# A linear attention and its feed-forward layers on one core: where the activation's last step writes, whose banks y and the state updates use, and a new order of the work

## The chip, the cores and the metric

The kernel runs on one core of a Trainium2 chip. The metric is the device time of one execution in microseconds (us), as a median of several runs; lower is better. A core has five engines, each with its own queue of instructions that it works off in order: PE (matrix products, with weight loads as PEld), DVE and POOL (elementwise), ACT (functions and copies) and SP (here it issues all transfers). They wait for one another by semaphores. Data lies in SBUF; PE writes its sums to PSUM, which has eight banks of 128 rows x 512 floats.

## What is computed

Attention with a decaying state per head, then a feed-forward pair of layers with an activation of its own:

```python
batch, n_heads, seq, head_dim = (4, 8, 768, 48)
...
for t in range(S):
    kt, vt, rt = (k[:, :, t], v[:, :, t], r[:, :, t])
    cur = np.einsum('bhd,bhe->bhde', u[None] * kt, vt)
    y[:, :, t] = np.einsum('bhd,bhde->bhe', rt, state + cur)
    state = w[None, :, :, None] * state + np.einsum('bhd,bhe->bhde', kt, vt)
...
h = x @ w_in                      # x [3072, 384], w_in [384, 2048]
sp = np.maximum(h, 0.0) + np.log1p(np.exp(-np.abs(h)))
g = h * erf(sp)
return (g @ w_out).astype(np.float32)      # w_out [2048, 384]
```

x is y with the heads side by side. The weights come as 64-bit floats (the kernel sees them as int64).

## The kernel before

**Chunks and blocks.** The attention runs over 24 chunks of 128 tokens; chunk g belongs to batch g % 4, and chunks 4b to 4b+3 make up block b, 512 tokens (`TB`), of the six blocks of the layers. For a chunk, PE multiplies r and k, which were scaled by powers of w (`prep_r` L222, `prep_k` L218), to A in two banks (`a_step`, PE at L301); DVE copies the masked A into `am` (L309, for chunks 0 and 1 L314) over a diagonal that comes from r, u and k (`diag_a` L263, `diag_b` L266, `diag_c` L270, `diag_m`); PE makes y from `am`, v and the state `sbd` (`y_product`, PE at L330) and the state's update ds from k and v (`ds_product`, PE at L353; k is scaled for it by `prep_n`, L226); DVE adds ds into the state (`s_add` L366, L368) and `s_mul` (L372) multiplies the state by the decay. `x_hi` (ACT, L375) and `x_lo` (DVE, L378; for some chunks ACT, L392) copy y as a high and a low part into x. Chunks 0 and 1 are "direct": they load less (below), POOL or DVE makes their product r*k (`prep_g`, L231), PE turns k (`turn_k`), and DVE makes the diagonal from that (`diag_v`, L253).

**Layers.** 96 layer steps n, each 128 hidden units (f) of one block: units 0 to 7 for blocks 0 and 1, then 8 to 15 for these, then 16 for each of blocks 2 to 5. Of each step, f1 is nine matmuls into a bank h of pool `ps3` (`f1`, PE at L411: high x high, high x low, low x high, three times); then a (ACT, tanh, L418), b (ACT, tanh, L422), z (DVE, L427), c, d, e (ACT, L431, L435, L439), g (DVE, L443), h (ACT, the high part `gh`, L449), l (DVE, the low part `gl`, L454), and f2, called p in the order, nine matmuls into the three sums `acc` (PE at L471).

**Weights.** Each of the two matrices comes in eight pieces of 768 columns (`WG`; 768 KB each). A piece takes six steps, `load_w` a to f: a on ACT (L123, from the raw words into the one buffer `wt`), b, c, d on DVE (L125, L127, L130, bits into `wt`), e on ACT (L133, the high part), f on DVE or POOL (L135, the low part). There is one buffer `wt` (`WTB`), so a piece's a waits for the f of the piece before it; there are two buffers for the raw words.

**PSUM.** `ps1` holds the three sums, `psa` two banks (tag "A"), `ps3` three (tag "h"). For chunks 0 to 3, y lies in a bank of `ps1` and ds in one of `ps3`; from chunk 4 on both lie in `psa`, where A lies too (but for chunks 0 and 2, whose A is in `ps3`). Banks of a pool are given out in turn, so a new tile waits for the last use of the tile that had its bank.

**What sets the order.** A string `ORDER` of tokens, one for each step: within the scheduler's manual mode each engine works its instructions off in the order of the tokens. L is the load of a chunk (a: r and k, 512 KB; b: the rest, 608 KB, of the direct chunks 224 KB), U that of u (192 KB), F the fetch and C the steps of a weight piece (C13d: `w_out`, piece 3, step d), R, K, N, G, Q and M the preparations of a chunk, V turn_k, A, P (masked copies), Y, D (ds), X and S as above; f, a, b, z, c, d, e, g, h, l, p with the number of the layer step; O the copy and store of sums, W dummy matmuls that keep PE busy, Z the count below, T, t, B and H the tables of powers of w. A "+" behind a token puts it on POOL, a "*" on ACT. SP issues the loads in the same order, all in one queue.

**The count.** `count_bad` compares w with its range (DVE), sums the differing entries with a tiny matmul (PE) and reduces that (DVE); the count decides, behind everything, whether a general version of the kernel runs after (it doesn't with these inputs).

The activation's last step before:

```python
def act_g(n):
    h = ff[n]["h"]
    nc.vector.scalar_tensor_tensor(out=h, in0=ff[n]["s"], scalar=FC, in1=h, ...)
```

## Time and profile before

| | us |
|---|---|
| three runs | 513.9, 515.3, 515.69 |
| median | 515.3 |
| profiled execution, its own time | 513.87 |
| span in that profile | 511.8 |
| granted TensorE clock in it | 0.997 of full |

Busy in the profiled execution:

| engine | busy us | share | instructions |
|---|---|---|---|
| PE | 496.6 | 97% | 4476 |
| PEld | 391.8 | 77% | 4476 |
| DVE | 357.4 | 70% | 642 |
| ACT | 390.4 | 76% | 712 |
| POOL | 135.7 | 27% | 135 |

The span is from the first to the last recorded instruction; some 2 us of the execution lie around it. A row of a time line gives the start, how long the instruction took (or a run of like ones, "x24"), the engine, the line of the kernel, the operation and its tiles as out<-in, and in brackets how long the engine idled before it and what it waited for. A busy PE is not the same as PE at its peak, since matmuls overlap: their modelled ends reach into the next one's start.

### The profile page before, as it was taken

How to read it: one execution, taken by the hardware profiler on the slowest of the kernel's cores; microseconds unless marked ns; L12 is line 12 of the kernel's file. 1: busy time of each engine (PE TensorE's matmuls, PEld its weight loads, DVE VectorE, ACT ScalarE, POOL GpSimd, SP SyncE). 2: the span in 40 equal slices, each digit the busy share in tenths (PEclk: the TensorE clock that was granted, in tenths of full speed). 3: DMA queues.
4: the chain of work that ended last, by engine and by line, in shares of the span. 5: the costliest groups of instructions: out<-in, count | busy, mean ns of one | idle time of the engine just before them, and what ended most of it. 6: DMA issues, size and time to landing. Idle time of an engine off the chain costs nothing.

```text
span 511.8 us, 11055 instructions
## 1 busy us (share of the span) xinstructions
PE 496.6 (97%) x4476; PEld 391.8 (77%) x4476; DVE 357.4 (70%) x642; ACT 390.4 (76%) x712; POOL 135.7 (27%) x135
## 2 busy tenths in 40 slices
...
GB/s 276 363 195 119 249 125 62 243 176 153 224 12 42 2 260 96 131 20 73 2 1 215 49 1 86 97 36 167 22 131 1 1 2 3 41 22 0 0 1 67
DMA packets 13993, 48.16 MB, mean 94 GB/s; under 512 B 1776, under 2 KB 2160, under 8 KB 13936
## 3 DMA queue, kind: packets, MB, share of 16 engines
...
q14 instruction: 20, 0.16, 0.1%
...
## 4 chain that ended last, share of the span: by engine, by line
PE 85%; DVE 5%; DMA 4%; ACT 3%; SPq 1%; issue 1%; ACTq 0%
PE acc L471 38%; PE h L411 37%; PE y L330 6%; PE A L301 3%; DMA out_dram<-o 2%; DMA raw<-in_win_dram 1%; PE ds L353 1%; DMA att<-in_att_dram 1%; DVE wt L130 1%; DVE wt L127 1%; DVE am L309 1%; DVE gl L454 1%; ACT s L435 0%; SPq L72 0%; ACT s L422 0%
## 5 line engine op out<-in xcount | busy, mean ns | idle before, releaser
L411 PE MATMUL h<-x,wih 128*128 128x512 f32 x576 | 184.8, 402 | 1.0 <-DVE gl L454 0.9
L411 PEld LDWEIGHTS h<-x,wih 128*128 128x128 f32 x576 | 106.4, 188 | 29.3 <-DVE gl L454 3.2
L471 PE MATMUL acc<-gh,woh 128*128 128x512 f32 x288 | 116.0, 403 | 0.0
L411 PE MATMUL h<-x,wil 128*128 128x512 f32 x288 | 114.3, 397 | 0.0
L471 PE MATMUL acc<-gh,wol 128*128 128x512 f32 x288 | 114.2, 397 | 0.0
L471 PE MATMUL acc<-gl,woh 128*128 128x512 f32 x288 | 114.1, 396 | 0.0
L427 DVE SCALAR_TENSOR_TENSOR s<-s,h 128x512 f32<-128x512 f32 x96 | 65.2, 683 | 46.8 <-ACT s L422 46.2
L454 DVE TENSOR_TENSOR gl<-h,gh 128x512 fp32r<-128x512 f32 x96 | 66.0, 689 | 39.8 <-ACT gh L449 38.3
L443 DVE SCALAR_TENSOR_TENSOR h<-s,h 128x512 f32<-128x512 f32 x96 | 66.0, 691 | 37.9 <-ACT s L439 37.3
L449 ACT CAST gh<-h 128x512 fp32r<-128x512 f32 x96 | 55.8, 582 | 36.1 <-DVE h L443 20.6
L418 ACT ACTIVATE s<-h 128x512 f32<-128x512 f32 x96 | 56.9, 593 | 27.5 <-PE h L411 27.1
L431 ACT ACTIVATE s<-s 128x512 f32<-128x512 f32 x96 | 60.0, 627 | 22.7 <-DVE s L427 22.4
L471 PEld LDWEIGHTS acc<-gh,woh 128*128 128x128 f32 x288 | 54.2, 188 | 14.2 <-issue 0.8
L411 PEld LDWEIGHTS h<-x,wil 128*128 128x128 f32 x288 | 54.3, 188 | 13.3 <-DVE wil L135 0.3
L471 PEld LDWEIGHTS acc<-gh,wol 128*128 128x128 f32 x288 | 54.3, 188 | 13.1
L471 PEld LDWEIGHTS acc<-gl,woh 128*128 128x128 f32 x288 | 54.3, 189 | 12.5
L422 ACT ACTIVATE s<-s 128x512 f32<-128x512 f32 x96 | 60.4, 630 | 1.7
L435 ACT ACTIVATE s<-s 128x512 f32<-128x512 f32 x96 | 60.4, 630 | 1.7
L439 ACT ACTIVATE s<-s 128x512 f32<-128x512 f32 x96 | 60.1, 629 | 1.7
L283 POOL TENSOR_TENSOR am<-idents,q 128x512 f32<-128x512 f32 x25 | 28.5, 1150 | 76.6 <-PE y L330 65.5
L309 DVE COPY_PREDICATED am<-mask,A 64x128 f32<-64x128 uint32 (+2 forms) x108 | 38.3, 389 | 3.0 <-PE A L301 1.9
L222 POOL TENSOR_TENSOR att<-att,wr 112x512 f32<-112x512 f32 x16 | 21.8, 1363 | 42.8 <-DMA att<-in_att_dram 42.8
...
## 6 DMA issues: line engine op xcount, KB each, us to landing
...
```

The source lines that it names most:

```text
L309: nc.vector.copy_predicated(out=o, data=ap[rows, n, :, i], mask=mask[rows, n, None, i].to_broadcast(list(o.shape)).bitcast(U32))
L411: nc.tensor.matmul(out=h, lhsT=w[:, f, q, :], rhs=x[:, xi, q, :], start=k == 0, stop=k == 8)
L418: nc.scalar.activation(out=s1, in_=e["h"], func=AF.Tanh, bias=FB0, scale=FA0)
L422: nc.scalar.activation(out=s1, in_=s1, func=AF.Tanh, bias=FB1, scale=FA1)
L427: nc.vector.scalar_tensor_tensor(out=e["s"], in0=e["s1"], scalar=FG, in1=e["h"], op0=ALU.mult, op1=ALU.add)
L431: nc.scalar.activation(out=s, in_=s, func=AF.Tanh, bias=FB2, scale=FA2)
L435: nc.scalar.activation(out=s, in_=s, func=AF.Square, bias=FB3, scale=FA3)
L439: nc.scalar.activation(out=s, in_=s, func=AF.Square, bias=FB4, scale=FA4)
L443: nc.vector.scalar_tensor_tensor(out=h, in0=ff[n]["s"], scalar=FC, in1=h, op0=ALU.subtract, op1=ALU.mult, reverse0=True)
L449: nc.scalar.copy(out=e["gh"], in_=e["h"])
L454: eng.tensor_tensor(out=e["gl"], in0=e["h"], in1=e["gh"].bitcast(F32), op=ALU.subtract)
L471: nc.tensor.matmul(out=acc[e], lhsT=w[:, f, es], rhs=g, start=first and i == 0, stop=last and i == 2)
```

## The change

Five things change. Step g writes its result over `s` in SBUF, in place of its bank h; steps h and l read it there. y of chunk 4 and later, and ds of all chunks, lie in `ps3` beside the layers' h, in place of `psa`. The first piece of `w_in` is fetched and split in two halves of 384 columns (tokens F00 and F08, C00 and C08), in the same raw and `wt` buffers. The count is split in three tokens (Z0a, Z0b, Z0c). And `ORDER` is another string: it has the same steps, but their sequence differs nearly everywhere, and several of a chunk's preparations, several weight steps f and some masks change between DVE, POOL and ACT. The diff, cut:

```diff
+    halves = {int(x[1]) for x in ORDER.split() if x[0] == "F" and x[2] == "8"}
+
+    def columns(which, g):
+        if which in halves and g in (0, 8):
+            return 0, slice(0, WG // 2) if g == 0 else slice(WG // 2, WG)
+        return g, slice(g * WG, (g + 1) * WG)
 
     def fetch_w(which, g):
-        raws[which, g] = raw = stage.tile([P, WG], I64, tag="raw", name=f"raw{which}{g}")
-        nc.sync.dma_start(out=raw, in_=(wout if which else win)[:, g * WG:(g + 1) * WG])
+        n, s = columns(which, g)
+        if n == g:
+            raws[which, n] = stage.tile([P, WG], I64, tag="raw", name=f"raw{which}{n}")
+        nc.sync.dma_start(out=raws[which, n][:, s.start - n * WG:s.stop - n * WG],
+                          in_=(wout if which else win)[:, s])
 
     bits = {}
 
     def load_w(part, eng, which, g):
-        words = raws[which, g].bitcast(I32).rearrange("p (n two) -> p n two", two=2)
+        n, s = columns(which, g)
+        own = slice(s.start - n * WG, s.stop - n * WG)
+        words = raws[which, n][:, own].bitcast(I32).rearrange("p (n two) -> p n two", two=2)
         wl, wh = words[:, :, 0], words[:, :, 1]
-        if part == "a":
-            bits[which, g] = stage.tile([P, WG], I32, tag="wt", name=f"wt{which}{g}", bufs=WTB)
-        t = bits[which, g]
+        if part == "a" and n == g:
+            bits[which, n] = stage.tile([P, WG], I32, tag="wt", name=f"wt{which}{n}", bufs=WTB)
+        t = bits[which, n][:, own]
...
         s["y"] = y_product(chunks[g], [s["am", 0], s["am", 1]], g % 4, g < 4, f"y{g}", g in direct,
-                           (ps1, f"acc{g % 2}") if g < 4 else (psa, "A"))
+                           (ps1, f"acc{g % 2}") if g < 4 else (ps3, "h"))
...
-    def ds_product(t, first, name):
-        ds = (ps3 if first else psa).tile([PR, NPAIR, D], F32, tag="h" if first else "A", name=name)
+    def ds_product(t, home, name):
+        ds = home[0].tile([PR, NPAIR, D], F32, tag=home[1], name=name)
...
     def act_g(n):
-        h = ff[n]["h"]
-        nc.vector.scalar_tensor_tensor(out=h, in0=ff[n]["s"], scalar=FC, in1=h, op0=ALU.subtract, op1=ALU.mult,
+        s = ff[n]["s"]
+        nc.vector.scalar_tensor_tensor(out=s, in0=s, scalar=FC, in1=ff[n]["h"], op0=ALU.subtract, op1=ALU.mult,
                                        reverse0=True)
 
     def act_h(n):
         e = ff[n]
         e["gh"] = fp.tile([P, TB], F32R, tag="gh", name=f"gh_{n}")
-        nc.scalar.copy(out=e["gh"], in_=e["h"])
+        nc.scalar.copy(out=e["gh"], in_=e["s"])
 
     def act_l(n, eng):
         e = ff[n]
         e["gl"] = fp.tile([P, TB], F32R, tag="gl", name=f"gl_{n}")
-        eng.tensor_tensor(out=e["gl"], in0=e["h"], in1=e["gh"].bitcast(F32), op=ALU.subtract)
+        eng.tensor_tensor(out=e["gl"], in0=e["s"], in1=e["gh"].bitcast(F32), op=ALU.subtract)
...
+    def count_bad(part):
+        if part == "a":
+            bad_["in"] = bad = const.tile([PR, NPAIR], F32, name="bad")
+            nc.vector.tensor_tensor(out=bad, in0=wp[:, 0, 0], in1=wc, op=ALU.not_equal)
+        elif part == "b":
+            bad_["out"] = cnt = psa.tile([1, NPAIR], F32, tag="A", name="cnt")
+            nc.tensor.matmul(out=cnt, lhsT=wr[:, 0, 0:1], rhs=bad_["in"], start=True, stop=True)
+        else:
+            nc.vector.tensor_reduce(out=fi, in_=bad_["out"], axis=AX.X, op=ALU.max)
...
-            st_.setdefault(num, {})["ds"] = ds_product(chunks[num], num < 4, f"ds{num}")
+            st_.setdefault(num, {})["ds"] = ds_product(chunks[num], (ps3, "h"), f"ds{num}")
...
-P101 g26 M111+ f28 a28 p24y p24z b28 z28 h26 l26 z27 c27 d27 p25 A11 f29 e27 a29 P110 P111 Y11 D11 g27 h27 l27 c28 d28
...
+p26 f29 a29 M110+ N11+ M111+ g28 Y10 D10 A11 h28 b29 h27 L12a L12b O232c S10a S10b l27 z29 f30 X10a c29 a30 b30 d29
```

Three places of the sequence follow; numbers behind a tile's name tell tiles of one name apart, except that `wt03` is piece 3 of `w_in`, `wt12` piece 2 of `w_out`, and so on, `h0`, `s1_0`, `s2_0`, `gh_0`, `gl_0` belong to layer step 0, and `att4`, `am4`, `A4` to chunk 4.

DVE at the first piece of `w_in`, before (chunks 0 to 3 around it):

```order
L314 TENSOR_TENSOR am0_0_217<-A0_0_191,mask_99 128x512
L314 TENSOR_TENSOR am0_1_219<-A0_1_192,mask_99 128x512
L127 SCALAR_TENSOR_TENSOR wt00_186<-raw00_172,wt00_186 128x768
L253 TENSOR_TENSOR att0_167<-att0_167,kt0_202 128x4x48 x2
L130 SCALAR_TENSOR_TENSOR wt00_186<-raw00_172,wt00_186 128x768
L253 TENSOR_TENSOR att1_170<-att1_170,kt1_237 128x4x48 x2
L314 TENSOR_TENSOR am1_0_249<-A1_0_224,mask_99 128x512
```

and after:

```order
L137 SCALAR_TENSOR_TENSOR wt00_185<-raw00_176,wt00_185 128x384
L273 TENSOR_TENSOR att2_172<-att2_172,ub_90 128x384
L140 SCALAR_TENSOR_TENSOR wt00_185<-raw00_176,wt00_185 128x384
L145 TENSOR_TENSOR wil_95<-wt00_185,wih_94 128x384
L263 TENSOR_TENSOR att1_169<-att1_169,kt1_232 128x4x48 x2
L376 TENSOR_TENSOR sbd_147<-ds0_277,wp_114 48x4x48 x2
L324 TENSOR_TENSOR am1_0_330<-A1_0_298,mask_99 128x512
L324 TENSOR_TENSOR am1_1_332<-A1_1_299,mask_99 128x512
L135 TENSOR_SCALAR wt00_185<-wt00_185 128x384
```

Before, one b, c, d of 768 columns stand there, and the piece's f comes later, with ten rows between its d and it; now steps b, c, d of the first half (384 columns) stand there, its f (L145) is the next instruction after its d (L140), and the second half's b comes after two masked copies of chunk 1.

DVE around the first g and l of the layers, before:

```order
L226 TENSOR_TENSOR att4_406<-att4_406,wkn_146 128x384
L309 COPY_PREDICATED am4_0_543<-mask_99,A4_0_580 128x512
L309 COPY_PREDICATED am4_1_545<-mask_99,A4_1_581 128x512
L443 SCALAR_TENSOR_TENSOR h0_570<-s2_0_621,h0_570 128x512
L427 SCALAR_TENSOR_TENSOR s2_1_671<-s1_1_666,h1_598 128x512
L427 SCALAR_TENSOR_TENSOR s2_2_676<-s1_2_673,h2_625 128x512
L454 TENSOR_TENSOR gl_0_680<-h0_570,gh_0_678 128x512
L309 COPY_PREDICATED am5_0_608<-mask_99,A5_0_641 128x512
```

and after:

```order
L276 TENSOR_TENSOR att6_541<-att6_541 128x384
L453 SCALAR_TENSOR_TENSOR s2_0_625<-s2_0_625,h0_580 128x512
L437 SCALAR_TENSOR_TENSOR s2_1_671<-s1_1_666,h1_610 128x512
L135 TENSOR_SCALAR wt01_674<-wt01_674 128x768
L137 SCALAR_TENSOR_TENSOR wt01_674<-raw01_544,wt01_674 128x768
L140 SCALAR_TENSOR_TENSOR wt01_674<-raw01_544,wt01_674 128x768
L464 TENSOR_TENSOR gl_0_685<-s2_0_625,gh_0_680 128x512
L232 TENSOR_TENSOR att6_541<-att6_541,wr_115 112x512
```

The g of step 0 (L443, now L453) wrote `h0` and now writes `s2_0`; its l (L454, now L464) reads `h0` and `gh_0` before, `s2_0` and `gh_0` after. Before, the z of steps 1 and 2 stand between them; now one z and three steps of weight piece 1.

ACT from the instruction behind the high part of piece 2 of `w_out` (the twelfth piece; L133, `woh`) to the first step of piece 3 (the thirteenth; L123), before:

```order
L418 ACTIVATE s1_7_1070<-h7_1059 128x512
L422 ACTIVATE s1_7_1070<-s1_7_1070 128x512
L431 ACTIVATE s2_6_1053<-s2_6_1053 128x512
L449 CAST gh_5_1116<-h5_951 128x512
L435 ACTIVATE s2_6_1053<-s2_6_1053 128x512
L439 ACTIVATE s2_6_1053<-s2_6_1053 128x512
L375 CAST x1_755<-y7_1081 128x3x128
L431 ACTIVATE s2_7_1114<-s2_7_1114 128x512
L435 ACTIVATE s2_7_1114<-s2_7_1114 128x512
L439 ACTIVATE s2_7_1114<-s2_7_1114 128x512
L449 CAST gh_6_1165<-h6_1024 128x512
L123 ACTIVATE wt13_1169<-raw13_1047 128x768
```

and after, from that high part (L143) on:

```order
L143 CAST woh_96<-wt12_1111 128x768
L441 ACTIVATE s2_6_1136<-s2_6_1136 128x512
L428 ACTIVATE s1_7_1152<-h7_1101 128x512
L432 ACTIVATE s1_7_1152<-s1_7_1152 128x512
L445 ACTIVATE s2_6_1136<-s2_6_1136 128x512
L428 ACTIVATE s1_8_1158<-h8_1141 128x512
L449 ACTIVATE s2_6_1136<-s2_6_1136 128x512
L133 ACTIVATE wt13_1161<-raw13_1127 128x768
```

Before, eleven instructions stand between the two; now six do: the steps of layer step 6 (c, d, e), of 7 (a, b) and the a of step 8.

## Rows read from the trace of the kernel before

**Rows 1.** The page's busy time of each engine, and traffic in its 40 slices.

```profile
PE 496.6 (97%) x4476; PEld 391.8 (77%) x4476; DVE 357.4 (70%) x642; ACT 390.4 (76%) x712; POOL 135.7 (27%) x135
...
GB/s 276 363 195 119 249 125 62 243 176 153 224 12 42 2 260 96 131 20 73 2 1 215 49 1 86 97 36 167 22 131 1 1 2 3 41 22 0 0 1 67
```

**Rows 2.** Stretches: us, busy time (count) of PE, PEld, DVE, ACT, POOL, PE clock, DMA.

```profile
30.00:60.00 30.00, 26.05 (x395) 19.25 (x396) 28.94 (x48) 25.12 (x48) 16.34 (x12) 1.00 0.54 192
60.00:85.00 25.00, 25.00 (x183) 19.78 (x183) 21.54 (x31) 21.38 (x37) 15.11 (x13) 1.00 0.37 128
...
110.00:500.00 390.00, 389.80 (x3213) 310.85 (x3212) 255.96 (x460) 302.20 (x544) 84.06 (x83) 1.00 0.18 63
```

**Rows 3.** Time line of PE: start, us, line, operation, [idle before <-releaser].

```profile
52.71 0.73 PE L411 MATMUL h<-x,wih 128*128 128x512 f32 x2 [0.79 <-DVE gl L454]
...
56.42 0.86 PE L330 MATMUL y<-att,sbd 112*32 112x128 f32 x24 [0.86 <-DVE am L309]
...
58.09 0.50 PE L471 MATMUL acc<-gh,woh 128*128 128x512 f32 x1
...
66.20 0.40 PE L411 MATMUL h<-x,wil 128*128 128x512 f32 x1
...
84.45 0.39 PE L471 MATMUL acc<-gh,woh 128*128 128x512 f32 x1
...
88.76 0.90 PE L301 MATMUL A<-att 48*64 48x128 f32 x32
```

**Rows 4.** Time line of DVE and of POOL: the weights' last steps.

```profile
64.83 1.08 DVE L135 TENSOR_TENSOR wil<-wt,wih 128x768 fp32r<-128x768 f32 x1
...
82.57 1.84 POOL L135 TENSOR_TENSOR wol<-wt,woh 128x768 fp32r<-128x768 f32 x1 [3.50 <-ACT woh L133]
```

**Rows 5.** Time line of ACT and of DVE: where the weights' steps waited.

```profile
10.35 0.90 ACT L123 ACTIVATE wt<-raw 128x768 f32<-128x768 f32 x1 [3.85 <-DMA raw<-in_win_dram]
...
11.28 0.56 DVE L125 TENSOR_SCALAR wt<-wt 128x768 int32<-128x768 int32 x1 [0.93 <-ACT wt L123]
...
60.23 0.69 DVE L125 TENSOR_SCALAR wt<-wt 128x768 int32<-128x768 int32 x1 [0.75 <-ACT wt L123]
...
75.06 0.55 DVE L270 TENSOR_REDUCE q<-att 128x8 f32<-128x384 f32 x1 [0.44 <-POOL att L266]
```

**Rows 6.** Time line of POOL and DVE: instructions that overlap, and two that don't.

```profile
17.37 1.59 POOL L218 TENSOR_TENSOR att<-att,wk 112x512 f32<-112x512 f32 x1
...
17.75 1.63 DVE L266 TENSOR_TENSOR att<-att 128x384 f32<-128x384 f32 x1
...
21.00 0.55 DVE L266 TENSOR_TENSOR att<-att 128x384 f32<-128x384 f32 x1
21.46 0.95 DVE L135 TENSOR_TENSOR wil<-wt,wih 128x768 fp32r<-128x768 f32 x1
...
57.41 1.84 POOL L135 TENSOR_TENSOR wol<-wt,woh 128x768 fp32r<-128x768 f32 x1
...
57.47 0.69 DVE L454 TENSOR_TENSOR gl<-h,gh 128x512 fp32r<-128x512 f32 x1
...
67.02 1.21 DVE L125 TENSOR_SCALAR wt<-wt 128x768 int32<-128x768 int32 x1
```

**Rows 7.** Groups by form: line, count | busy us, mean ns | idle before, releaser.

```profile
L443 DVE SCALAR_TENSOR_TENSOR h<-s,h 128x512 f32<-128x512 f32 x96 | 66.0, 691 | 37.9 <-ACT s L439 37.3
...
L454 DVE TENSOR_TENSOR gl<-h,gh 128x512 fp32r<-128x512 f32 x96 | 66.0, 689 | 39.8 <-ACT gh L449 38.3
...
L427 DVE SCALAR_TENSOR_TENSOR s<-s,h 128x512 f32<-128x512 f32 x96 | 65.2, 683 | 46.8 <-ACT s L422 46.2
...
L366 DVE TENSOR_TENSOR sbd<-ds,wp 48x192 f32<-48x192 f32 x8 | 2.8, 353 | 0.2
...
L435 ACT ACTIVATE s<-s 128x512 f32<-128x512 f32 x96 | 60.4, 630 | 1.7
...
L449 ACT CAST gh<-h 128x512 fp32r<-128x512 f32 x96 | 55.8, 582 | 36.1 <-DVE h L443 20.6 <-PE acc L471 10.7 <-DVE sbd L368 4.1
```

137 lines of the change are left out of this document (66 added, 71 removed).

## The prediction, made before the changed kernel was run

> **What bounds the kernel now.** I read the page's list of engines first: PE is busy for 496.6 of 511.8 us [rows 1]. Then the table of stretches: from 60 us on PE has no idle time worth the name, 25.00 of 25 us, and 389.80 of 390 us between 110 and 500 us, while DVE and ACT are at 66 and 77% there [rows 2]. So from about 60 us the end is fixed: what PE still has to do then, back to back, plus the tail of copy and store. The change takes no matmul of the layers or of the attention away and adds none (the dummy matmuls are also the same in number), so it can move the end in two ways alone: PE gets into its unbroken run with more or less work behind it, or a hole opens in the run.
>
> Ahead of the run DVE is the busy one, 28.94 of 30 us between 30 and 60 us [rows 2]. PE's row shows how they hang together: at 52.71 layer step 4 waited 0.79 us for DVE's last step of an earlier one (its bank), at 56.42 the y of chunk 6 waited 0.86 us for a masked copy on DVE, and from 58.09 on it goes back to back [rows 3], with no hole over 0.3 us that I found. But three hand-overs after that arrive with nothing to spare. DVE's weight step of 64.83 ends at 65.91, and PE's first matmul on that low part starts at 66.20; POOL's last weight step of 82.57 ends at 84.41, and p6, whose third matmul reads it at about 84.9, starts at 84.45 [rows 3, 4]. So PE and the chain through DVE, ACT and POOL walk in step until p6. I take p6 as the cut: where it starts in the changed kernel, with how much of PE's work done, gives the end.
>
> **The activation's last step.** Step g (L443) writes SBUF in place of its bank. A DVE step with the same inputs that writes SBUF is z: 683 ns against g's 691 [rows 7]. Nothing. Step h on ACT now reads SBUF: 582 ns today; ACT's steps from SBUF to SBUF take 630 [rows 7], so some 0.05 us more, 96 times 4.6 us on an engine that idles for over 100 us; in the chains ahead of p6, six times, 0.3 us, spread over places where ACT is not last. A layer's bank is free after g, not after h and l: some 0.58 + 0.69 us and the waits between them earlier. That removes the 0.79 us at 52.71, but next in line stands the masked copy of 56.42 [rows 3], which does not move by it, so I count nothing.
>
> Step l on DVE (L454) is the delicate one: it had one input in PSUM, now both are in SBUF. First what the trace shows. DVE's L266, both inputs in SBUF, takes 0.55 us at 21.00, but 1.63 at 17.75, where POOL was inside an instruction of 17.37 that itself took 1.59; it lost 1.08 us. At 67.02 a weight step took 1.21 where the same step at 11.28 takes 0.56 [rows 5]. The l of 57.47, one input in PSUM, ran wholly inside POOL's 1.84 us of 57.41 and took its usual 0.69 [rows 6]. So l joins the instructions that POOL can hold up. Ahead of the cut I count 2.7 us of such losses in the trace: the 1.08, the 0.65 of 67.02 and five smaller, on some 48 DVE instructions that could be hit. In the change these are about 58 (six l steps and four others more), while POOL, by the same sum of what moves, has a sixth less work by then: 2.7 x 58/48 x 0.83 = 2.7 us. I count no difference, with bounds: 0.5 if DVE is mostly first, 6 if each l and each multiplication that meets POOL loses as L266 did.
>
> The Trainium skill (SBUF — State Buffer, Who interferes with whom) says the same as a rule, and it speaks against this change: a DVE instruction with two SBUF inputs and a GpSimd instruction that reads SBUF shut each other out for a whole instruction, and whichever starts first wins; with at most one SBUF input DVE is free of it. The trace agrees on both kinds (1.63 against 0.69). By the rule taken at its worst the upper bound above is the sum, and the kernel slower.
>
> **The order, and the weights' first piece.** Each piece of 768 weights goes through one buffer: ACT, three steps on DVE, ACT, and a last step on DVE or POOL. At 60.23 DVE waited 0.75 us for the ACT step that could not begin before POOL had let go of the buffer [rows 5]. In halves the first piece costs three DVE starts more, some 0.1 us, and lands differently: ahead of its first half now stand 2176 KB against 1248 KB ahead of the whole one, so 2560 KB must be in against 2016. At the 363 GB/s of the page's second slice that is 1.5 us later than today's 10.35 [rows 1, 5]; the step on ACT is half as long, and DVE has two masked copies and two multiplications of chunk 2 ahead of its own, which end near 12.3. Today DVE waited 0.93 there [rows 5]; I expect no wait.
>
> Ahead of the thirteenth piece's last step (that which p6 needs) DVE's work changes so. Ten multiplications or sums of a chunk go, twelve come, mostly larger: with instructions following each other about 0.08 us closer than they are long (21.00 to 21.46 for 0.55 [rows 6]) they take 0.47 for 384 columns and, by l's 0.69 [rows 7], some 0.62 for 512: +1.5 us. Four state updates come and two go, 2 x 0.36 = +0.7 [rows 7]. One weight step of 0.87 (0.95 less 0.08 [rows 6]) and half a piece's go to POOL, -1.3. One g and one l fall behind the cut, -1.2. With the halves +0.1: together -0.2, equal.
>
> Waits on DVE ahead of the cut: today 0.93, 0.75 and 0.44 [rows 5], 2.1. In the new order, by following the rows: 0.3 until chunk 1's first half has landed; 0.65 for the first half-piece's last step, which stands directly behind its third and needs ACT, where two copies of keys stand first, which wait for PE's turn of chunk 1, which waits for a product now made on POOL; 0.3 at the first g; 0.35 at the twelfth piece's last step, now on DVE behind ACT; and about 1.6 around g6, whose ACT steps stand among six others. Sum 3.2, so +1.1; bounds 2 and 4.5. On ACT the thirteenth piece's cast is due behind shorter work than today, where it came some 0.7 us after DVE was done, -0.6.
>
> **Sum at the cut.** p6 at 84.45 - 0.2 + 1.1 - 0.6 + 0 = 84.75. PE has by then the same layers, y and A done and one state update more, half a microsecond of work: 84.95 today. Gain 0.2 us, bounds +3.5 (no losses to POOL, no waits) and -4 (both at their worst).
>
> **y and state updates in the layers' banks.** Three banks now hold the layers' h, and y and ds of chunk 4 and later. No row shows such a wait. The nearest are the bank waits of 52.71 (0.79) [rows 3] and, as bound from below, nothing, since g gives its bank back earlier. The place with least cover is f30: h29, y10 and ds10 fill the banks, and only A11 lies between ds10 and f30; two updates on DVE (0.35 each, [rows 7]) and their start must fit under the 0.90 us of an A (88.76 [rows 3]), in a DVE queue whose other steps last 0.69. I give 0.3 us, 0 to 0.7 there. The other such places (f46, f80) have 2 us of cover for 1.5 us of work. Sum for the run 0.3, up to 1.5. Against it stands that A no longer shares its two banks with y and ds; in the run no A waited for them, so nothing.
>
> The count in three steps moves 0.3 us of work on DVE and one tiny matmul on PE: nothing. The late store of the fifth block has only SP's queue around it: nothing.
>
> **Rivals.** *Equal* (my forecast): +0.2 - 0.3, so 513.87 + 0.1 = 514.0 for an execution like the profiled one. That one lies at the low end of the runs (513.9, 515.3, 515.69; the median 1.4 above it); as median I put 514.7. *Faster*: DVE loses next to nothing to POOL and meets half the waits I named; p6 starts near 82.3, 2.6 us gained, 512.1 as median. For it: POOL has less to do, the buffer chain from piece 12 to 13 has fewer ACT steps in between. Against: DVE is as full of work as before. *Slower by the port*: from the point where four more DVE steps ahead of p6 lose what L266 lost, 4 x 1.08 = 4.3 us, less 0.2: 518.8; half of it 516.8. For it: l and four more DVE steps are now such, and l then holds POOL too, whose last weight steps p2, f2, f4 and p6 wait for. Against: l with POOL idle, as behind piece 11, loses nothing. *Slower by banks*: where the 36 y and ds tiles each cost a tenth of a microsecond, 3.6 us, 518.3; it decides from the point where DVE's queue is longer than PE's cover, which in the run, with DVE two thirds busy, is rare. That the earlier bank is worth nothing, since PE waited for one only once, is part of the forecast.
>
> **How the numbers follow.** Forecast 0.46, faster 0.28, slower by the port 0.16, slower by banks 0.10. A tenth or so of the forecast's weight lies beyond its edges either way; 0.3%, 1.5 us, is what a measurement can tell. So faster 0.30, same 0.45, slower 0.25. The range runs from the faster case at its bound (3.5 us less) to between the two slower ones at half: 511.2 to 517.6.
>
> **What would show it.** Right: PE's last wait lies between 55 and 85 us and p6, in equal work, starts within 1.5 us of today's; DVE's l takes 0.69 save where POOL runs, then up to 1.7. Wrong: PE idle behind 110 us by more than 1 us in sum (banks), or DVE's instructions with two SBUF inputs all at their usual length and PE's unbroken run beginning 2 us earlier in equal work.

## The result, and the profile after

The changed kernel takes 517.82 us (median of 6 runs, 517.3 to 519.37), the kernel before 514.32 beside it: ratio 1.0063, 95% interval 1.0047 to 1.0079. It is slower by some 3.2 us, where the prediction had 514.7 with a range up to 517.6 and called no change the likeliest. The profiled execution has a span of 515.5 us, 3.7 more than that of before (by the medians it is 3.5, by the ratio 3.2).

The list of engines on the page of after, to be held against [rows 1]: PE has the same work (497.6 against 496.6 us), but DVE is busy for 9.6 us more.

```profile
PE 497.6 (97%) x4476; PEld 393.4 (76%) x4476; DVE 367.0 (71%) x640; ACT 397.3 (77%) x730; POOL 142.5 (28%) x137
```

The table of stretches of after (columns as in [rows 2]) shows where PE stood still:

```profile
75.00:85.00 10.00, 9.74 (x42) 7.55 (x41) 8.63 (x13) 9.20 (x16) 0.94 (x1) 1.00 0.64 220
85.00:110.00 25.00, 23.51 (x98) 18.05 (x98) 23.05 (x30) 22.32 (x42) 10.71 (x9) 1.00 0.34 121
110.00:200.00 90.00, 88.05 (x829) 69.77 (x828) 76.25 (x129) 71.63 (x124) 32.99 (x29) 1.00 0.37 126
200.00:300.00 100.00, 100.00 (x884) 80.75 (x883) 65.22 (x120) 79.46 (x150) 38.84 (x38) 1.00 0.19 66
```

Between 75 and 200 us PE idles for 0.26 + 1.49 + 1.95 = 3.70 us; before, it idled 0.20 between 110 and 500 in all [rows 2] and nothing between 60 and 85. So the unbroken run, on which the prediction rested, is broken. That the sum is also the difference of the spans is chance: PE was late ahead of these holes already, and won some back behind them (both below). The two largest holes follow each other. First PE's time line, then DVE's, then POOL's, of after:

```profile
91.63 0.73 PE L421 MATMUL h<-x,wih 128*128 128x512 f32 x2 [0.78 <-DVE s L453]
...
94.71 0.72 PE L421 MATMUL h<-x,wih 128*128 128x512 f32 x2 [0.71 <-DVE s L453]
```

```profile
84.92 1.62 DVE L464 TENSOR_TENSOR gl<-s,gh 128x512 fp32r<-128x512 f32 x1
86.47 3.91 DVE L232 TENSOR_TENSOR att<-att,wr 112x512 f32<-112x512 f32 x1
90.30 0.68 DVE L437 SCALAR_TENSOR_TENSOR s<-s,h 128x512 f32<-128x512 f32 x1
```

```profile
84.06 1.93 POOL L145 TENSOR_TENSOR wol<-wt,woh 128x768 fp32r<-128x768 f32 x1 [17.35 <-ACT woh L143]
85.96 0.95 POOL L382 TENSOR_TENSOR sbd<-sbd,wp 48x192 f32<-48x192 f32 x1
86.87 1.01 POOL L236 TENSOR_TENSOR att<-att,wkn 128x384 f32<-128x384 f32 x1
87.85 1.98 POOL L273 TENSOR_TENSOR att<-att,ub 128x384 f32<-128x384 f32 x2
89.91 1.34 POOL L276 TENSOR_TENSOR att<-att 128x384 f32<-128x384 f32 x1
```

Lines are those of the changed kernel (g L453, l L464, z L437, `prep_r` L232). The scaling of r of chunk 8, on DVE, takes 3.91 us where the same step usually takes 0.69: both its inputs are in SBUF, and it stands still through four POOL instructions that follow each other without a break. It ends at 90.38, half a microsecond behind the second of the two products L273, and so it ran when these were done. The l ahead of it (84.92) had lost 0.93 us, but to one POOL instruction alone: it ends at 86.54, 0.55 us behind the end of the weight step of 84.06, and it is POOL's next, the state multiplication of 85.96, that then takes 0.95 us in place of 0.51. So the l got in between two POOL instructions that follow each other, and the scaling of r did not. Behind them in DVE's queue stand a z and a g; f11 and f12 wait for banks that g steps give back. The chain of waits of after says it in its own way: the hold-up counts as "issue", time in which the engine waited for nothing that the profile shows, and in the time line as a long instruction. No list of waits has it.

```profile
86.54 0.06 DVE att L232
86.60 3.70 issue
90.30 0.69 DVE s L437
```

The groups by form of after, against [rows 7]: l takes 794 ns in the mean (before 689), g 683 (691), the copy h 614 (582).

```profile
L464 DVE TENSOR_TENSOR gl<-s,gh 128x512 fp32r<-128x512 f32 x96 | 76.2, 794 | 36.5 <-ACT gh L459 35.2
...
L453 DVE SCALAR_TENSOR_TENSOR s<-s,h 128x512 f32<-128x512 f32 x96 | 65.4, 683 | 63.2 <-ACT s L449 63.0
...
L459 ACT CAST gh<-s 128x512 fp32r<-128x512 f32 x96 | 58.5, 614 | 23.0 <-DVE s L453 18.3 <-PE acc L481 4.6
```

Of the 96 l steps 16 are held up, by 10 us in sum: the longest is that of step 21, in DVE's time line:

```profile
149.78 2.71 DVE L464 TENSOR_TENSOR gl<-s,gh 128x512 fp32r<-128x512 f32 x1
```

By the time lines 19 DVE instructions of this trace take over 0.4 us more than others of their form while POOL works. 15 of them end as the l of 84.92 does, about their own length behind the end of the POOL instruction that they met. Four outlast at least one such end: the scaling of r, the l of step 21, one more l (282.17) and a scaling of k (337.68). What decides between the two is not shown.

At the cut that the prediction chose the changed kernel was late too. p6 starts at 86.47:

```profile
86.47 0.39 PE L481 MATMUL acc<-gh,woh 128*128 128x512 f32 x1
```

PE has done by then the same layers, y and A as before at 84.45 [rows 3], and one ds more, worth 0.5 us: 1.5 us late, where the prediction had 0.2 early. How much of the 1.5 us POOL's hold-ups cost is not shown: this trace also has 3.4 us at half the granted clock at 41 to 45 us (below), that of before none ahead of 500 us.

### The profile page after: what moved, and what is told of

Its sections match the earlier page's. It is cut to its first block, busy times and chain, and to the rows that moved or that the text cites. A ratio compares the mean times of both kernels' runs of the same rounds, so it can differ in the third digit from the quotient of the medians.

```text
span 515.5 us, 11059 instructions
## 1 busy us (share of the span) xinstructions
PE 497.6 (97%) x4476; PEld 393.4 (76%) x4476; DVE 367.0 (71%) x640; ACT 397.3 (77%) x730; POOL 142.5 (28%) x137
## 4 chain that ended last, share of the span: by engine, by line
PE 70%; DVE 17%; DMA 4%; ACT 4%; issue 3%; SPq 0%; DVEq 0%; ACTq 0%
PE acc L481 32%; PE h L421 31%; PE y L340 5%; DMA att<-in_att_dram 3%; DVE gl L464 2%; PE A L311 2%; DVE wt L137 2%; DVE wt L140 2%; DVE am L319 2%; DVE s L453 2%; DMA raw<-in_win_dram 2%; DVE s L437 1%; DVE wt L135 1%; PE ds L363 1%; DVE att L273 1%
## 5 line engine op out<-in xcount | busy, mean ns | idle before, releaser
L453 DVE SCALAR_TENSOR_TENSOR s<-s,h 128x512 f32<-128x512 f32 x96 | 65.4, 683 | 63.2 <-ACT s L449 63.0
L464 DVE TENSOR_TENSOR gl<-s,gh 128x512 fp32r<-128x512 f32 x96 | 76.2, 794 | 36.5 <-ACT gh L459 35.2
L437 DVE SCALAR_TENSOR_TENSOR s<-s,h 128x512 f32<-128x512 f32 x96 | 65.5, 684 | 25.7 <-ACT s L432 23.4
L459 ACT CAST gh<-s 128x512 fp32r<-128x512 f32 x96 | 58.5, 614 | 23.0 <-DVE s L453 18.3
L293 POOL TENSOR_TENSOR am<-idents,q 128x512 f32<-128x512 f32 x19 | 21.5, 1139 | 60.0 <-DVE q L280 48.1
L273 POOL TENSOR_TENSOR att<-att,ub 128x384 f32<-128x384 f32 x13 | 13.6, 1054 | 62.2 <-DMA att<-in_att_dram 62.2
```

What stands on the lines that cost most here:

```text
L437: nc.vector.scalar_tensor_tensor(out=e["s"], in0=e["s1"], scalar=FG, in1=e["h"], op0=ALU.mult, op1=ALU.add)
L453: nc.vector.scalar_tensor_tensor(out=s, in0=s, scalar=FC, in1=ff[n]["h"], op0=ALU.subtract, op1=ALU.mult, reverse0=True)
L459: nc.scalar.copy(out=e["gh"], in_=e["s"])
L464: eng.tensor_tensor(out=e["gl"], in0=e["s"], in1=e["gh"].bitcast(F32), op=ALU.subtract)
```

## The experiments

Theory A: DVE steps with two SBUF inputs, l above all, are held up by POOL, and this is the loss. Rival B: the banks that y and the state updates now share with the layers. Rival C: the new order in itself. Rival D: what is lost early is covered by later waits anyway. Rivals E and F come up at single runs, in the expectations. Each run is compared with runs of the kernel before on the same chip; the ratio is the measure, since medians of different chips differ by up to 0.9 us for the kernel before.

Another rival is the granted clock, which differs from execution to execution of one kernel: of 83 runs of the kernel before beside these experiments, the 48 with a mean clock of 0.996 or more average 514.4 us, the 35 others 515.7. It doesn't explain the main comparison: the clock averages 0.9948 over the runs of the changed kernel, 0.9948 over those of after_r8_later, 0.9954 over those of the kernel before beside it.

| kernel | median us | ratio to before | 95% interval |
|---|---|---|---|
| after_r8_later | 515.0 | 1.0009 | 0.9988 to 1.0029 |
| after_r8_on_pool | 516.07 | 1.0033 | 1.0019 to 1.0048 |
| after_g_in_bank | 608.25 | 1.1793 | 1.1762 to 1.1825 |
| before_g_in_sbuf | 523.84 | 1.0175 | 1.0161 to 1.0189 |
| before_l_two_sbuf | 523.83 | 1.0167 | 1.0143 to 1.0192 |
| after_pool_writes | 508.72 | 0.9894 | 0.9868 to 0.9919 |
| before_pool_writes | 512.55 | 0.9954 | 0.9940 to 0.9967 |
| before_g_sbuf_pool_writes | 512.81 | 0.9952 | 0.9935 to 0.9969 |
| after_r8_whole_piece | 518.91 | 1.0074 | 1.0055 to 1.0094 |
| after_q6_later | 517.21 | 1.0039 | 1.0026 to 1.0052 |
| after_r8_q6 | 515.12 | 1.0003 | 0.9989 to 1.0016 |
| after_r8_q6_s4s7 | 514.03 | 0.9992 | 0.9978 to 1.0006 |
| after_start_of_layers | 515.85 | 1.0032 | 1.0019 to 1.0045 |
| after_y8_later | 517.0 | 1.0056 | 1.0041 to 1.0071 |
| after_k6_later | 516.08 | 1.0017 | 1.0001 to 1.0032 |
| after_k6_h0_s4 | 518.55 | 1.0063 | 1.0039 to 1.0086 |

### One token: the scaling that took 3.91 us

```diff
-z8 h7 l7 R8 C13f+ S6c+ f9 a9
+z8 h7 l7 C13f+ S6c+ f9 a9
...
-c10 h9 l9 C05d a11
+c10 h9 l9 R8 C05d a11
```

> The changed kernel with one token moved: DVE's scaling of r of chunk 8 (line 232) stands behind the l of step 9 instead of behind the l of step 7. In the changed kernel it started at 86.47 us and took 3.91 us in place of 0.69, while POOL ran five instructions back to back, and PE then stood 0.78 us at 91.63 and 0.71 us at 94.71 for two g steps. Theory A (a DVE instruction with two SBUF inputs is held up for as long as POOL goes from one instruction to the next, and this one is on the path): the instruction takes 0.7 to 1.4 us at its new place, both holes of PE go, and the time falls by 1.3 to 1.8 us to about 516.2. Rival B (those steps were late anyway, by the banks that y and the state updates now share): the holes stay or move by less than a microsecond, time 517.3 to 518.3.

The ratio falls from 1.0063 to 1.0009: some 2.8 us, give or take 1.3 by the two intervals (2.1 by the spans of the two traces). Theory A had 1.3 to 1.8, and the two holes are 1.49. At its new place the step takes its usual time, and PE is without a break from 85 to 110 us (its time line of DVE, its table of stretches):

```profile
93.92 0.68 DVE L232 TENSOR_TENSOR att<-att,wr 112x512 f32<-112x512 f32 x1
```

```profile
85.00:110.00 25.00, 25.00 (x108) 20.11 (x107) 21.90 (x31) 24.39 (x46) 10.70 (x9) 1.00 0.34 120
```

Theory A holds here and B is not needed: with homes and banks as they are, one token takes the measurable loss away. In PE's time the gain is 2.0 us by f12 (94.71 against 92.74) and 2.3 by f28 (169.69 against 167.43), for equal work. Rival C is right in one point: the scaling of r had two SBUF inputs before the change too, on POOL; it is the new order that put it on DVE, beside POOL's row. The other losses are still there: p6 starts at 86.42 in this run, and PE idles 1.95 us between 110 and 200 us as in the changed kernel; what the order wins elsewhere (below) covers them.

The same step on POOL, where the kernel before has it:

```diff
-z8 h7 l7 R8 C13f+ S6c+ f9 a9
+z8 h7 l7 C13f+ R8+ S6c+ f9 a9
```

> The changed kernel with chunk 8's scaling of r on POOL, directly behind the weight piece 3 of w_out, as the kernel before has it. Theory A (it is DVE's wait for POOL that costs, not the work itself): DVE's queue goes on, the holes at 91 and 94 us go, POOL's row of instructions grows by 1.3 to 1.7 us with nothing late behind it; time as after_r8_later, 514.5 to 515.5. Rival F (any step with two SBUF inputs that stands there, the z or l behind it, is held instead, since POOL goes on longer): the l of step 9 or a weight step is held 1 us or more, and the time stays at 516.5 or above.

516.07 lies between what the two had said, and its interval overlaps that of after_r8_later. Rival F is right about the place: POOL's row is now 1.7 us longer, and it is the next l, that of step 8, which stands through it. DVE's time line, then POOL's, of this run:

```profile
88.97 2.01 DVE L464 TENSOR_TENSOR gl<-s,gh 128x512 fp32r<-128x512 f32 x1 [1.14 <-ACT gh L459]
```

```profile
88.44 1.99 POOL L273 TENSOR_TENSOR att<-att,ub 128x384 f32<-128x384 f32 x2
90.51 1.35 POOL L276 TENSOR_TENSOR att<-att 128x384 f32<-128x384 f32 x1
```

PE's two holes are gone all the same, but for 0.14 us between 85 and 110. PE starts p6 0.63 us earlier than in after_r8_later and ends its last matmul 0.39 us later; 0.3 of this 1.0 us is lost by f12, 0.6 between f40 and f60, far from the edit. So, as far as one trace of each can tell, what costs is not the step itself, but which two-input step of DVE meets POOL's row, and who waits behind it.

### The activation's last step alone, in the order of before

```diff
-        e["s"] = fp.tile([P, TB], F32, tag="s2", name=f"s2_{n}")
+        e["s"] = fp.tile([P, TB], F32, tag="s2", name=f"s2_{n}", bufs=3)
...
-        nc.vector.scalar_tensor_tensor(out=h, in0=ff[n]["s"], scalar=FC, in1=h, op0=ALU.subtract, op1=ALU.mult,
+        nc.vector.scalar_tensor_tensor(out=s, in0=s, scalar=FC, in1=ff[n]["h"], op0=ALU.subtract, op1=ALU.mult,
...
-        nc.scalar.copy(out=e["gh"], in_=e["h"])
+        nc.scalar.copy(out=e["gh"], in_=e["s"])
...
-        eng.tensor_tensor(out=e["gl"], in0=e["h"], in1=e["gh"].bitcast(F32), op=ALU.subtract)
+        eng.tensor_tensor(out=e["gl"], in0=e["s"], in1=e["gh"].bitcast(F32), op=ALU.subtract)
```

> The kernel before with the activation's part of the change alone: g writes SBUF, h and l read it there; since s now lives until l, its tiles have three buffers in place of two. Order, banks, first piece and count as before. Theory A (the port): the l steps that overlap POOL, 27 of 96 in the trace of before, lose up to 0.4 us each, 5 to 10 us of DVE time in sum, and since DVE is on the path only up to about 85 us and in a few places later, the time rises by 0.5 to 2.5 us: 515 to 517. Rival C (the new order alone costs the time): l is slowed as much, but nothing waits for it; the time stays at 514.3 within 0.5, or falls a little, since the banks come free earlier.

8.7 us slower, more than theory A had said. To see whether it is l's second SBUF input and nothing else, g and h were left in the bank and l alone was changed:

```diff
-        eng.tensor_tensor(out=e["gl"], in0=e["h"], in1=e["gh"].bitcast(F32), op=ALU.subtract)
+        eng.tensor_tensor(out=e["gl"], in0=e["gh"].bitcast(F32), in1=e["gh"].bitcast(F32), op=ALU.subtract)
```

> The kernel before with one operand of l changed: l subtracts gh from itself, so both its inputs are in SBUF and the low part of the activation is left out (zeros go into the matmuls in its place). g and h work in the bank as before, all buffers and the order are those of before; the bank is free after h. before_g_in_sbuf took 523.8 against 515.2. Theory A (l's second SBUF input, by POOL, is the whole of these 8.7 us): l loses some 20 us in sum again, and the time is 522 to 525. Rival E (the third buffer for s, or g and h in SBUF, cost part of it): 515 to 519.

The same 523.8. The groups by form of the two runs, first before_g_in_sbuf:

```profile
L454 DVE TENSOR_TENSOR gl<-s,gh 128x512 fp32r<-128x512 f32 x96 | 87.5, 914 | 39.1 <-ACT gh L449 37.2
```

```profile
L454 DVE TENSOR_TENSOR gl<-gh 128x512 fp32r<-128x512 f32 x96 | 89.0, 930 | 36.8 <-ACT gh L449 35.4
```

l takes 21.5 and 23 us more than in [rows 7], with its two SBUF inputs as the only thing in common. So in the order of before the change of l costs 8.7 us, and rival E (the third buffer for s, or g and h in SBUF, as part of the cost) falls. The granted clock averages 0.991 and 0.989 in these two against 0.995 and 0.996 beside them, so some 1 us of the 8.7 may be the clock's, an estimate from the two groups of runs above.

### POOL made to write and hardly to read

```diff
+    class Writes:
+        @staticmethod
+        def tensor_tensor(out, in0, in1, op):
+            one = lambda t: t[(slice(None),) * (len(t.shape) - 1) + (slice(0, 1),)]
+            nc.gpsimd.tensor_tensor(out=one(out), in0=one(in0), in1=one(in1), op=op)
+            nc.gpsimd.memset(out.bitcast(F32) if out.dtype == F32R else out, 0.0)
...
-        eng = {"+": nc.gpsimd, "*": nc.scalar}.get(x[-1], nc.vector)
+        eng = {"+": Writes, "*": nc.scalar}.get(x[-1], nc.vector)
```

> The changed kernel with each elementwise product or difference on POOL cut to its last column index 0 and followed by a fill of the same tile with zeros: POOL still waits for the same work, but hardly reads SBUF. The products and low parts made by POOL are left out. Theory A (POOL's reading of SBUF holds DVE): the l steps take 0.69 us throughout, line 232 at 86 too, and PE's holes between 75 and 170 go; POOL also hands on its results earlier, so this is a lower bound of what is to be had: 511 to 514. Rival (the steps are held by something else, POOL's writing or transfers): l as long as now, 516 or above.

> before_g_in_sbuf with POOL's products and differences cut and filled in the same way (left out of the result). It took 523.8 with POOL reading. Theory A: l back to 0.69 us, time at or below that of the kernel before, 511 to 515, that is 9 us or more less. Rival: 519 or above.

> The kernel before with POOL's products and differences cut and filled in the same way (left out of the result). It has lost 2.7 us to POOL ahead of 85 us by my count. Theory A: 512 to 514.5, as POOL's results come earlier too. Against after_pool_writes and before_g_sbuf_pool_writes this tells what the new order, the halves and the earlier bank are worth where POOL holds nothing up: if the earlier bank is worth nothing, before_g_sbuf_pool_writes is within 0.7 us of it.

All three as theory A has it, the first even below its 511 to 514. The products and low parts that POOL makes are left out in them, so their results are others. The groups by form, first of after_pool_writes, then of before_g_sbuf_pool_writes: with POOL still at work (its fills take 0.3 to 0.7 us each), but hardly reading, l and the scaling are at their usual length. 13 l steps of the first and 19 of the second overlap a fill, and none of these takes over 0.73 us.

```profile
L464 DVE TENSOR_TENSOR gl<-s,gh 128x512 fp32r<-128x512 f32 x96 | 66.1, 688 | 38.8 <-ACT gh L459 37.4
...
L232 DVE TENSOR_TENSOR att<-att,wr 112x512 f32<-112x512 f32 x13 | 8.9, 683 | 0.0
```

```profile
L454 DVE TENSOR_TENSOR gl<-s,gh 128x512 fp32r<-128x512 f32 x96 | 66.2, 691 | 43.0 <-ACT gh L449 41.0
```

They also price the rest. Without POOL's reading, g in SBUF is worth nothing in the order of before (512.81 against 512.55); the new order with the halves and the shared banks is worth 512.55 - 508.72 = 3.8 us (3.1 by the ratios). POOL's work costs the changed kernel 517.8 - 508.7 = 9.1 us, the kernel before 515.1 - 512.6 = 2.5. Part of each is that POOL hands on its results earlier in these runs, so each of the two figures is an upper bound of the hold-ups; their difference, 6.6 us (6.3 by the ratios), is an estimate and no bound. That the 6.6 less the 3.8 gives about the difference measured is arithmetic, since the same four times make up both, and no evidence of its own.

PE's holes behind 110 us go too: between 110 and 200 us it idles 0.14 us, against 1.95 in the changed kernel (table of stretches of after_pool_writes).

```profile
110.00:200.00 90.00, 89.86 (x840) 71.81 (x839) 70.10 (x127) 72.23 (x125) 25.36 (x73) 1.00 0.40 135
```

### The banks

85 of the steps with g back in the bank, in the new order (the other 11, numbers 5, 27, 28, 38, 43, 54, 57, 60, 61, 63 and 78, can't wait that long):

```diff
+KEEP = {0, 1, 2, 3, 4, 6, 7, 8, 9, 10, 11, 12, 13, 14, 15, 16, 17, 18, 19, 20, 21, 22, 23, 24, 25, 26, 29, 30, 31, 32, 33, 34, 35, 36, 37, 39, 40, 41, 42, 44, 45, 46, 47, 48, 49, 50, 51, 52, 53, 55, 56, 58, 59, 62, 64, 65, 66, 67, 68, 69, 70, 71, 72, 73, 74, 75, 76, 77, 79, 80, 81, 82, 83, 84, 85, 86, 87, 88, 89, 90, 91, 92, 93, 94, 95}
...
-        s = ff[n]["s"]
-        nc.vector.scalar_tensor_tensor(out=s, in0=s, scalar=FC, in1=ff[n]["h"], op0=ALU.subtract, op1=ALU.mult,
+        e = ff[n]
+        e["g"] = e["h"] if n in KEEP else e["s"]
+        nc.vector.scalar_tensor_tensor(out=e["g"], in0=e["s"], scalar=FC, in1=e["h"], op0=ALU.subtract, op1=ALU.mult,
```

> The changed kernel, but in 85 of the 96 layer steps g writes its bank again, and h and l read it there, as before the change (the steps 5, 27, 28, 38, 43, 54, 57, 60, 61, 63 and 78 keep SBUF: with the new order they can't wait for a bank that long). Theory A (l's second SBUF input puts it behind POOL): l's mean falls from 794 ns to 690 to 710 in these steps, its total from 76.2 to about 67 us; the 2.63 us of the l at 149.86 become 0.69, PE's holes at 151 (0.9), 156 and 168 shrink, and the time falls by 1 to 2 us, to about 516.3; the 3.91 us of line 232 at 86 stay. Rival B (banks are what PE lacks): held 1.3 us longer, they make PE wait in more places, and the time rises to 518.5 or above.

Theory A's time is far off, though l is back at 688 ns: 608 us. PE's list of waits (us in all, times, longest) shows what the order needs the early bank for:

```profile
PE h L421 <- DVE gl L465: 45.6, 29, 3.5
PE ds L363 <- DVE gl L465: 6.3, 4, 3.6
PE y L340 <- DVE gl L465: 5.4, 3, 2.8
```

So the two parts hang together: the new order counts on a bank that g frees, and frees a bank only by handing l a second SBUF input. The homes of y and ds could not be changed back alone, in either order, since each then waits for something that stands behind it; that is read from the order, and no run shows it. Moving one such wait out of the way (the y of chunk 8, which waited 0.6 us):

```diff
-M90+ Y8 z25 h23 l23 X8a c25 d25 b24 X8b z24 M91+ e25 c24 M100+ d24 p22 p23x
+M90+ z25 h23 l23 c25 d25 b24 z24 M91+ e25 c24 M100+ d24 p22 Y8 X8a X8b p23x
```

> As after_start_of_layers, and y of chunk 8 stands behind p22 instead of ahead of it, with its two copies. It waited 0.6 us there for the g of step 23, whose bank it takes. Theory B (banks shared by y and layers cost PE here and there): that wait goes, 0.5 us less than after_start_of_layers, if nothing else comes late. Rival: the two copies of y now come late for ACT and DVE, and the gain is 0 or a loss up to 1 us.

It is 1.1 us slower than the kernel it was made from (after_start_of_layers, below), not faster. PE's wait for that g is gone, but it now waits 0.9 us for a high part of the weights from ACT, and 0.7 us for a copy of y on DVE: the rival's way.

### The first piece in halves

after_r8_later with F08 and the six tokens C08a to C08f+ taken out, which makes F00 and C00a to C00f the whole piece:

```diff
-L0a L1a L1b L2a L0b U0 F00 L2b L3a L3b F08 B0* C00a B0
+L0a L1a L1b L2a L0b U0 F00 L2b L3a L3b B0* C00a B0
```

> after_r8_later with the first piece of w_in whole again, fetched and split at the places of the first half. The prediction gave the halves +0.1 us of DVE starts, a landing 1.5 us later than before the change and a wait of 0.65 us at the first half's low part. If the halves are worth something, DVE and PE wait for the whole piece (768 KB must be in, 384 KB more, 1.1 us at 363 GB/s) and the time rises by 0.5 to 1.5 us over 515.0; if PE's hand-overs until 60 us are set elsewhere, it stays within 0.5 us of it.

518.91 against 515.0: in this order the halves are worth 3.9 us (3.3 by the two ratios), where the prediction had them at a cost of 0.1, and the expectation of this run at 1.5 at most. The granted clock averages 0.991 in these runs against 0.995, so some of this may be the clock's. With the piece whole DVE waits 1.17 us for its first step and 0.90 for its last, which POOL then holds for another 1.05 (DVE's time line of this run); masked copies of chunk 1 stand behind it, and PE waits 3.7 us for them.

```profile
13.54 0.56 DVE L135 TENSOR_SCALAR wt<-wt 128x768 int32<-128x768 int32 x1 [1.17 <-ACT wt L133]
...
17.74 2.00 DVE L145 TENSOR_TENSOR wil<-wt,wih 128x768 fp32r<-128x768 f32 x1 [0.90 <-ACT wih L143]
```

```profile
PE tp L208 <- DVE am L324: 3.7, 1, 3.7
```

### What was lost ahead of 60 us

In the changed kernel the diagonal of chunk 6 (L273) took 2.08 us at 37.29 (2.00 of it at 37.38 in the chain of waits), ahead of two masked copies; y of chunk 4 waited 1.75 us for these, until 40.07, and behind it the granted clock was halved, as the table of stretches shows:

```profile
42.00:44.00 2.00, 2.00 (x44) 1.04 (x37) 1.93 (x4) 1.67 (x4) 0.00 (x0) 0.50 0.27 33
```

```diff
-S3c S3d C10d N4 z0 Q6a P40 P41 Y4 Q6b C10e C10f+
+S3c S3d C10d N4 z0 P40 P41 Q6a Y4 Q6b C10e C10f+
```

> The changed kernel with one token moved: the first multiplication of chunk 6's diagonal on DVE (line 273) stands behind the two masked copies of chunk 4 instead of ahead of them. In the changed kernel it started at 37.38 us and took 2.00 us in place of 0.55, beside a weight step and a scaling on POOL; the copies came late, PE stood 1.75 us until 40.07, and from 41 to 45 us the granted clock was 0.50. Theory A (that hold-up and the slower clock behind it are on the path): PE's wait at 40 falls under 0.5 us, the clock stays at 1.00, and of some 3 us won there 0.7 to 2 reach the end: about 516.5. Rival D (PE waits for DVE until about 60 us anyway, and DVE does the same work): the wait goes, the clock stays up, and the time stays within 0.5 of 517.8.

517.21, a ratio of 1.0039 against 1.0063: by the ratios some 1.2 us, about what theory A had said, but the intervals overlap, so it is not clear of noise. The wait that was to go only changed its place. POOL's next instruction now holds the second product of that diagonal (L276, 1.51 us), behind it stands the g of step 0, and the ds of chunk 4 waits for its bank:

```profile
PE ds L363 <- DVE s L453: 1.8, 1, 1.8
```

In this trace the granted clock stayed up all the same (its table of stretches):

```profile
42.00:44.00 2.00, 2.00 (x36) 0.98 (x34) 1.93 (x3) 1.97 (x4) 0.00 (x0) 1.00 0.42 86
```

Together with the moved scaling of r it adds nothing:

> The changed kernel with both tokens moved (chunk 8's scaling of r behind the l of step 9, chunk 6's diagonal behind the masked copies of chunk 4). Moving the first alone gave 2.8 us, the second alone 1.2. Theory A (two separate hold-ups of DVE by POOL, one after the other on the same path): the gains add up, 517.8 - 2.8 - 1.2 = 513.8, ratio to the kernel before 0.998. Rival D (what is won at 40 us waits at the next hand-over again once the hole at 90 is gone): no better than the first alone, 515.0.

Rival D fits here. Next the l of step 21, with two state multiplications of POOL out of its way:

```diff
-C14f+ p14 p15x
+C14f+ S4c+ S7c+ p14 p15x
...
-C16f+ S7c+ S4c+ R9+ f24
+C16f+ R9+ f24
```

> As after_r8_q6, and POOL's two state multiplications (line 382, chunks 4 and 7) moved ahead, from behind the weight piece 6 of w_out to behind its piece 4, where POOL is idle for 6 us. In the run with the first token moved the l of step 21 started at 147.52 and took 2.71 us in place of 0.69 beside these two and a scaling of r; ACT then waited 1.58 us for the z behind it, and PE 0.74, 1.2 and 0.7 us between 150 and 156. Theory A: l takes 1.3 to 2.0 us, PE's waits there fall from 2.6 to 1.3 us or less, and the time falls by 0.7 to 1.5 us more, to about 512.7. Rival (the scaling alone holds l up as long, or the waits have another cause): within 0.4 us of after_r8_q6.

514.03: this l is no longer held (the product ahead of it on DVE is, instead, by 1.2 us), and the median is 1.1 us lower than without, though the two intervals overlap. It is the best version found, and not to be told from the kernel before (0.9978 to 1.0006). Three more attempts started from it (the third from the second), at the stretch ahead of 60 us:

```diff
-b1 g0 z1 K6+ C01a c1 d1 X4a h0 C01b C01c C01d l0 R6
+b1 g0 h0 z1 C01a c1 d1 X4a l0 C01b C01c C01d R6
...
-C01f+ f2 f3
+C01f+ K6+ f2 f3
```

> As after_r8_q6_s4s7 (514.0), with three more tokens moved where the layers begin: h and l of step 0 stand right behind its g and behind the next z, ahead of three weight steps on DVE, and POOL's scaling of k of chunk 6 stands behind the weight piece 1 of w_in. In after_r8_q6_s4s7 the scaling made DVE's line 276 of 39.20 last 1.51 us in place of 0.55, g then made ds of chunk 4 wait 1.81 us, and l came at 44.28, so that p0 began at about 45.2, behind matmuls at a clock of 0.50. Theory A (what DVE loses to POOL there goes through to the end): PE's wait for g falls under 1 us, p0 begins 1.5 to 2.5 us earlier, and of that 0.5 to 2 us reach the end: 512.0 to 513.5, ratio to before 0.994 to 0.997. Rival D (the next hand-overs of DVE, ACT and POOL until 90 us take it back): new waits of PE between 47 and 90 us of the same sum, time 513.7 to 514.3.

p0 began 2.5 us earlier (42.71 against 45.18), as said, but the time is worse than either theory had said: what was won came back as two new waits, PE's for the state updates and DVE's for a product of POOL (PE's list of waits, DVE's time line):

```profile
PE h L421 <- DVE sbd L378: 1.8, 2, 1.4
```

```profile
55.29 0.55 DVE L280 TENSOR_REDUCE q<-att 128x8 f32<-128x384 f32 x1 [1.42 <-POOL att L276]
```

Only the scaling of k moved, and then h, l, ds and the state updates of chunk 4 with it:

```diff
-g0 z1 K6+ C01a c1
+g0 z1 C01a c1
...
-S4d+ R7+ Q7b+
+S4d+ R7+ K6+ Q7b+
```

> As after_r8_q6_s4s7 (514.0), with one more token moved: POOL's scaling of k of chunk 6 stands behind its scaling of r of chunk 7 (some 10 us later) instead of directly behind the weight piece 0 of w_out. At 39.20 it made DVE's line 276 last 1.51 us in place of 0.55, behind which stood g of step 0. after_pool_writes gained 4 us on the kernel before by 60 us. Theory A (these hold-ups just ahead of PE's unbroken run carry most of that): g comes 0.9 us earlier, PE's wait of 1.81 us at 41 falls to 0.9, and 0.5 to 1 us reaches the end: 513.0 to 513.6. Rival D (PE's start at 45 us hangs on the three weight steps between g and l, and what is won waits again): within 0.4 us of 514.0.

```diff
-g0 z1 C01a c1 d1 X4a h0 C01b C01c C01d l0 R6 C01e e1 D4 W2 A5 W2 p0x p0y p0z S4b Q6c S4a P50
+g0 h0 z1 C01a c1 d1 X4a l0 D4 C01b C01c S4b S4a C01d R6 C01e e1 W2 A5 W2 p0x p0y p0z Q6c P50
```

> As after_k6_later, and h and l of step 0 ahead of three weight steps, and the state updates of chunk 4 (whose ds holds a bank) ahead of the last of these. In after_start_of_layers (515.9, which had the first two, the scaling of k at another place) p0 began 1.5 us earlier, but f3 then waited 1.35 us for the state updates, and DVE 1.42 us for a product of POOL at 55. Theory A: with the updates early and POOL's queue in the old order both waits go; PE runs from 44 us without a break, equal work 1 to 2 us earlier at 60, and the time is 512.3 to 513.5, ratio to before 0.994 to 0.997. Rival D: other waits between 47 and 70 us take the place, 513.7 to 515.

In these two the A of chunk 6 reads k ahead of its scaling, so that part of the result is another, and A has one wait less than it should. Both are slower than after_r8_q6_s4s7 all the same, and than either theory had said (516.08 and 518.55): A waits for another chunk's scaling, f1 for x_lo. By f4 after_pool_writes is 4.6 us ahead of the changed kernel (52.30 against 56.93). Which of the hold-ups ahead of it carry this stays open; taken away one by one by order alone, they come back as other waits.

## Why the prediction was wrong

The predicted sum had the gains and the losses of the change both near nothing. They are of some size: an estimated 6 us more lost to POOL, 3 to 4 won by the order. The measured 517.82 lies only 0.2 us above the range; that it came so near is luck, since two large terms of opposite sign were both taken as small. Term by term:

- **The earlier bank: right.** It was counted at nothing, and 512.81 against 512.55 bears it out for the order of before. But the new order uses it, as 608 us without it show, and so it is not free to be taken back.
- **l's second input: a mis-sized term.** "2.7 x 58/48 x 0.83 = 2.7 us", no difference, with 0.5 to 6 as bounds. Ahead of p6 DVE's instructions lost 5.9 us in the changed kernel, each held against the usual length of its form (4.8 of it between 20 and 40 us, 0.93 on an l), and 2.5 in the kernel before: 3.4 us more, and just inside the upper bound. Two things were wrong with the unit. A hold-up was taken as the rest of one POOL instruction (L266's 1.08 [rows 6]); most are, but four of the 19 over 0.4 us outlast the end of one or more, and the longest stands through four. And the average of before was carried over, an average of an order in which l could not be held, so that POOL's work stood freely beside it: the kernel before with the new l alone loses 21.5 us on DVE and 8.7 in time. What l's second input alone costs in the new order no run shows.
- **p6 as the cut: the step that failed.** The prediction took it that behind p6 nothing but the banks could open holes, since PE ran unbroken there [rows 2]. It put the l steps, "one g and one l fall behind the cut", and with them the scaling of r of chunk 8, out of the sum. Moving that one scaling, the third DVE instruction behind the l that p6 waits for, takes away 2.8 of the 3.2 us (give or take 1.3, as above). A run without holes in the trace of before says that every hand-over there had some slack, not how much; f11's was used up by a hold-up of 3.2 us.
- **The order: too small.** Equal work (-0.2) and 1.1 us of waits were forecast. With POOL's reading gone the new order, halves and banks win 3.8 us (3.1 by the ratios); in that order 3.3 to 3.9 hang on the halves, which were priced at their starts and their landing alone, and not at the masked copies behind the whole piece.
- **The banks for y and ds: too small, within the bound.** 0.3 us, up to 1.5. Of the 1.95 us that PE idles between 110 and 200 us, 0.7 and 0.4 are waits of y and f1 for a bank that g or a state update held (list of waits of after). So the prediction's own sign of being wrong, over 1 us idle behind 110 us, came. But it had put this down to the banks alone, and with POOL hardly reading, in the same banks, only 0.14 us are left.
- **A term that was missing:** something brings back part of what the holes cost. At f30, where both kernels have done equal work on PE, the changed one is 5.3 us late (PE's time lines, after and then before); at PE's last matmul it is 3.8.

```profile
186.08 0.71 PE L421 MATMUL h<-x,wih 128*128 128x512 f32 x2
```

```profile
180.74 0.63 PE L411 MATMUL h<-x,wih 128*128 128x512 f32 x2
```

From f30 on PE changes 30 times between attention and layers in the changed kernel and 50 times in the kernel before, for the same matmuls. If that is the reason, a change costs some 0.08 us, an estimate; no run has this alone.

The rival "slower by the port" was the right one, with 516.8 to 518.8, and had 0.16. Its deciding point, "four more DVE steps ahead of p6 lose what L266 lost", 4.3 us, came in part: 3.4 us more were lost there. But p6 was late by 1.5 us only, and the loss that one edit takes away lay behind it.

The Trainium skill (SBUF — State Buffer, Who interferes with whom) names the pair of instructions that shut each other out, and the runs agree: two SBUF inputs on DVE against an instruction of POOL that reads SBUF, and with POOL's reading cut the l takes 688 ns again beside its fills. The prediction gave this rule without one condition: where the Trainium skill says there that a DVE instruction with at most one SBUF input does not contend, it leaves out DVE's 2-port modes, and it names tensor_scalar among the instructions that can enter them; the weight step of 67.02, a TENSOR_SCALAR with one SBUF input, took 1.21 us in place of 0.56 [rows 5, 6]. The Trainium skill says too (same page, SBUF: two separate sides) that whichever starts first has the port for a whole instruction. The l of 84.92 agrees. But the DVE step that waited at 86.47 did not get in when POOL's instruction ended at 86.91, nor at the end of the next, 87.88: there the measurement goes further than the Trainium skill, and the length of POOL's unbroken row is what the step can cost at worst.
